# The last batch of a long-convolution kernel: its inverse transform cut by time instead of by channel

## The chip, the cores and the metric

The kernel runs on one core of a Trainium2 chip. The metric is the device time of one execution, in microseconds.

## The reference, cut to what matters

For each of 8 batches, linear attention without softmax on 8 heads of 64 channels over 576 positions, normalised by its root mean square, gives `x` (576 x 512). Then a gated long convolution:

```python
proj = x @ w_proj                                   # 512 -> 3 * 512
x1, x2, x3 = proj[..., :D], proj[..., D:2*D], proj[..., 2*D:]
X2 = np.fft.rfft(x2, n=S, axis=1)                   # S = 576
H = np.fft.rfft(filter_fft, n=S, axis=0)[None]
x2_conv = np.fft.irfft(X2 * H, n=S, axis=1)
out = (x1 * x2_conv * x3) @ w_out                   # float32, 8 x 576 x 512
```

## The kernel before

Matrices are bf16, sums and output float32. Both transforms are matrix multiplications with tables made on the chip. The spectrum of a batch is `Y`, six tiles of frequencies by 512 channels: three groups g (0, 1, 2), each with two parts h (0 even, 1 odd). `fft(b, g)` makes group g: TensorE transforms, VectorE (DVE) multiplies with the filter's spectrum (L423, L424), and an add joins the halves: on GpSimd (POOL) for g = 1 (L426), on DVE through the returned function for g = 0 of batches 1 to 7 (L427); group 2 is one multiply (L432). `proj13` makes the gate `g13` = x1 * x3, four channel groups of 128 (matmuls L443, DVE multiply L449).

The inverse, `inv(b, dcs)`, works on channel groups `dcs` with channels on partitions and time along the free axis, in a fixed order: position c of 576 stands for block c // 64, and a block's 64 positions are rows three apart in time. For a channel group TensorE makes an odd and an even half of 288 columns in PSUM (192 from groups 1 and 2, L469; 96 from group 0, L471). ScalarE (ACT) copies the odd half to SBUF (L473), DVE adds and subtracts the halves (L475, the second one reversed, L478) into `u`, three more DVE steps over thirds of 192 (L481, L483, L482) give the convolution `w`, and a multiply with `g13` (L487) gives `yg`.

The output projection needs all 512 channels (`yg` of all four groups) of a block: `outp` does 256 positions (blocks 0 to 3, 4 to 7) in one PSUM tile (matmuls L505, ACT copy L513) and issues transfers of 256 KB from SyncE's queue (SP, L516); block 8 of two batches shares a tile (L509).

Batches overlap: while b is projected and inverted, b + 1 runs its attention. The last batch has none, and `last(b)` ends the kernel by another scheme: the inverse runs one channel group at a time, the two output tiles of the batch before stand between the groups, and then `out1` makes five tiles of 128 positions: first the mixed tile (block 8 of batches 6 and 7, L530), then blocks 0 and 1, 2 and 3, 4 and 5, 6 and 7 (L527). Each is evicted by ACT or DVE (L533) and leaves in two transfers of 128 KB, one on SP and one on POOL, SP or ACT's queue (L536).

PSUM is four rotating tiles of two banks (`ps_tile`); SBUF work tiles rotate by tag. The framework derives waits from tiles and regions, and its scheduler orders each engine's instructions.

Of the kernel before, what the change touches and what calls it, by code (L numbers as in the profile page):

```python
# [9 lines left out]
FP32 = mybir.dt.float32  # L10
BF16 = mybir.dt.bfloat16
# [4 lines left out]
P = 128  # L16
# [4 lines left out]
def kernel(  # L21
# [16 lines left out]
    nc = tc.nc  # L38
    B, H, S, D = q.shape
    DM = H * D  # L40
    D3 = 3 * DM
    assert (B, H, S, D) == (8, 8, 576, 64)
    SB = S // 3
# [12 lines left out]
    def ps_tile(name):  # L56
        return psp.tile([P, 2, 512], FP32, name=name, tag="ps")
# [345 lines left out]
    def fft(b, g):  # L403
        x2 = st[b]['x2']
        if g == 1:
            st[b]['Y'] = work.tile([P, 6, DM], BF16, name="Y", tag="Y")
        Y = st[b]['Y']
        xp = ps_tile("ps_X")
        mm = nc.tensor.matmul
        lo, hi = slice(0, 64), slice(64, P)  # L410
        if g < 2:
            n = N1 if g == 0 else P
            if g == 0:
                mm(xp[:n, 0], FW[0:96, 0, 0, 0:n], x2[0:96, 0], start=True, stop=True)
                for c in range(2):
                    mm(xp[:n, 1], FX[:, c, 0:n], x2[:, c], start=(c == 0), stop=(c == 1))
            else:
                for ri in range(2):
                    mm(xp[:, ri], FW[:, 0, 2 + ri], x2[:, 2 + ri], start=True, stop=False)
                mm(xp[:, 0], FW[lo, 1, 2], x2[lo, 4], start=False, stop=True)  # L420
                mm(xp[:, 1], FX[hi, 2], x2[hi, 4], start=False, stop=True)  # L421
            t_ = work.tile([P, 2, 2, DM], FP32, name="tpw", tag="tpw", bufs=2)
            nc.vector.tensor_mul(out=t_[:n, 0], in0=xp[:n], in1=HH[:n, g, 1:3])  # L423
            nc.vector.tensor_mul(out=t_[:n, 1], in0=xp[:n], in1=HH[:n, g, 0:2])  # L424
            if g or not b:
                nc.gpsimd.tensor_add(out=Y[:n, 2 * g:2 * g + 2], in0=t_[:n, :, 0], in1=t_[:n, :, 1])  # L426
            return lambda: nc.vector.tensor_add(out=Y[:n, 2 * g:2 * g + 2], in0=t_[:n, :, 0], in1=t_[:n, :, 1])  # L427
        for i, r in enumerate((lo, hi)):
            mm(xp[r, 0], FW[:, 0, 4 + i, r], x2[:, 2 + i], start=True, stop=False)
        mm(xp[lo, 0], FW[lo, 1, 4, lo], x2[lo, 4], start=False, stop=True)  # L430
        mm(xp[hi, 0], FX[hi, 3, hi], x2[hi, 4], start=False, stop=True)
        nc.vector.tensor_mul(out=Y[:, 4:6], in0=xp[:, 0:1].to_broadcast([P, 2, DM]), in1=HM)  # L432
# [18 lines left out]
    def inv(b, dcs):  # L451

        Y, g13 = st[b]['Y'], st[b]['g13']
        if dcs[0] == 0:
            st[b]['yg'] = work.tile([P, NDC, S], BF16, name="yg", tag="yg", bufs=3)
        m = len(dcs)
        if m == 2:
            po, pe = ps_tile("ps_invo"), ps_tile("ps_inve")  # L460
            p_ = (pe[:, :, 0:TH], po[:, :, 0:TH])
        else:
            pp = ps_tile("ps_inv")
            p_ = (pp[:, 0:1, 0:TH], pp[:, 1:2, 0:TH])
        for h in (1, 0):
            for i, dc in enumerate(dcs):
                cs = slice(dc * P, (dc + 1) * P)
                for g in (1, 2):
                    nc.tensor.matmul(p_[h][:, i, 0:SB], Y[:, 2 * g + h, cs], IV[:, 2 * g + h, 0:SB],  # L469
                                     start=(g == 1), stop=(g == 2))  # L470
                nc.tensor.matmul(p_[h][:, i, SB:TH], Y[:N1, h, cs], IV[:N1, h, 0:SB // 2], start=True, stop=True)  # L471
        os_ = work.tile([P, 2, TH], FP32, name="os", tag="os")[:, 0:m]
        nc.scalar.copy(out=os_, in_=p_[1])  # L473
        u = work.tile([P, 2, S], BF16, name="u", tag="u", bufs=2)[:, 0:m]
        add = nc.vector.tensor_add(out=u[:, :, 0:TH], in0=p_[0], in1=os_)  # L475
        if b == 0:
            tc.keep_in_program_order(add)
        nc.vector.tensor_sub(out=u[:, :, TH:S], in0=p_[0][:, :, ::-1], in1=os_[:, :, ::-1])  # L478
        w = work.tile([P, 2, S], BF16, name="w", tag="w", bufs=2)[:, 0:m]
        u3, w3 = (t.rearrange("p j (m r) -> p j m r", m=3) for t in (u, w))  # L480
        nc.vector.tensor_add(out=w3[:, :, 1], in0=u3[:, :, 0], in1=u3[:, :, 2])  # L481
        nc.vector.tensor_sub(out=w3[:, :, 1], in0=u3[:, :, 1], in1=w3[:, :, 1])  # L482
        nc.vector.tensor_add(out=w3[:, :, 0:3:2], in0=u3[:, :, 0:3:2], in1=u3[:, :, 1:2].to_broadcast([P, m, 2, SB]))  # L483
        d2 = slice(dcs[0], dcs[0] + m)

        def fin():
            nc.vector.tensor_mul(out=st[b]['yg'][:, d2], in0=w, in1=g13[:, d2])  # L487
        return fin
# [3 lines left out]
    def o_rows(b, *blks):  # L492
        t0 = [SB * (x // 3) + x % 3 for x in blks]
        two = [[(t0[1] - t0[0]) * DM, 2]] if len(t0) == 2 else []
        return bass.AP(tensor=out.tensor, offset=out.offset + (b * S + t0[0]) * DM, ap=[[3 * DM, 64]] + two + [[1, DM]])
# [21 lines left out]
                else:  # L517
                    nc.sync.dma_start(out=o_rows(b - 1 + i, NR - 1), in_=ot[64 * i:64 * i + 64, 0])

    def out1(b, c, ev, q1):  # L520

        yg = st[b]['yg']
        pp = ps_tile("ps_out")
        for dc in range(NDC):
            kw = dict(start=(dc == 0), stop=(dc == NDC - 1))
            if c < 4:
                nc.tensor.matmul(pp[:, 0], yg[:, dc, c * P:(c + 1) * P], wo[:, dc], **kw)  # L527
            else:
                for i, y in enumerate((yt[0], yg)):
                    nc.tensor.matmul(pp[64 * i:64 * i + 64, 0], y[:, dc, 4 * P:S], wo[:, dc], **kw)  # L530
        ot = work.tile([P, 2, DM], FP32, name="ot", tag="ot", bufs=3) if c < 3 else \
            work.tile([P, 2, 2, DM], FP32, name="ot_", tag="tpw", bufs=2)[:, 0]
        ev(out=ot[:, 0], in_=pp[:, 0])  # L533
        for i in range(2):
            bb, blk = (b, 2 * c + i) if c < 4 else (b - 1 + i, NR - 1)
            (q1 if i else nc.sync).dma_start(out=o_rows(bb, blk), in_=ot[64 * i:64 * i + 64, 0])  # L536

    def last(b):
        for dc in range(NDC):
            inv(b, (dc,))()  # L540
            if dc < 2:
                outp(b - 1, 2 * dc)
        act, dve = nc.scalar.copy, nc.vector.tensor_copy
        for c, ev, q1 in ((4, act, nc.gpsimd), (0, dve, nc.gpsimd), (1, act, nc.sync), (2, act, nc.scalar), (3, dve, nc.scalar)):
            out1(b, c, ev, q1)


    def warm(n):
# [22 lines left out]
    for b in range(B):  # L571
        nxt = b + 1 < B
        proj2(b)
        if b == 1:
            fins.append(inv(0, (2, 3)))
            fins[0]()
        if b:
            fins[1]()
        if b == 0:
            fold_filter()  # L580
            proj13(0, 0)
            proj13(0, 1)
            gen_h(1)
            gen_h(0)
            fft(0, 1)
            gen_h(2)
            qtr(1, (0,))
            fft(0, 0)
            qtr(1, (1,))
            fft(0, 2)  # L590
            kv(1)
        elif nxt:
            kv(b + 1)
            qtr(b + 1)
        if b + 2 < B:
            load_kv(b + 2, (0, 8))
            load_q(b + 2)
        if b == 0:
            proj13(0, 2)
            att_o(1, 0)  # L600
            att_o(1, 1)
            att_r(1, 0)
            att_r(1, 1)
            att_o(1, 2)
            proj13(0, 3)
            att_x(1, 0)
            fold(1, 0)
            att_o(1, 3)
            att_r(1, 2)
            att_r(1, 3)  # L610
            att_x(1, 1)
            fold(1, 1)
            fins = [inv(0, (0, 1))]
        for dc in range(NDC) if b else ():
            if dc < 3:
                add = fft(b, (1, 0, 2)[dc]) or add
            if nxt:
                att_o(b + 1, dc)
            proj13(b, dc)
            if dc == 2:  # L620
                add()
            if nxt:
                att_r(b + 1, dc)
                if dc % 2:
                    att_x(b + 1, dc // 2)
                    fold(b + 1, dc // 2)
            if b and nxt and dc in (1,):
                outp(b - 1, 2 * (1,).index(dc))
        if not nxt:
            last(b)  # L630
            continue
        if b:
            for c0 in (2, 4):
                outp(b - 1, c0)
            del st[b - 1]
            fins = [inv(b, (dp, dp + 1)) for dp in (0, 2)]
            fins[0]()
# [30 lines left out]
```

## Time and profile before

| | us |
|---|---|
| median of 6 runs (234.9 to 235.37) | 234.94 |
| the profiled execution's own time | 234.93 |
| its span, first to last instruction | 232.8 |
| busy: TensorE | 211.1 (91%) |
| busy: DVE | 196.0 (84%) |
| busy: ACT | 156.7 (67%) |
| busy: POOL | 70.5 (30%) |
| projections of the last batch end on TensorE (L443) | 214.09 |
| last multiply with the gate (L487) ends | 223.64 |
| last TensorE result | 225.85 |

All times below count from the start of the span. TensorE's clock was granted at 0.99 of full speed over the span. The engine shares are means over the whole kernel; the change is in the last twenty microseconds, and what counts there is read from that stretch.

### The profile page before, as it was taken

Reading aid. Unit: us, or ns where it says so; the run is one execution under the profiler, and the core shown is the slowest. Engines: PE = TensorE matmul, PEld = TensorE weight load, DVE = VectorE, ACT = ScalarE, POOL = GpSimd, SP = SyncE. Lnnn points to the kernel's source line nnn. Section 1 sums busy time; section 2 is a strip of 40 time slices with the busy share of each in tenths; the row PEclk is TensorE's granted clock in tenths of the full one; section 3 lists DMA queues with packets and bytes.
Section 4 is the critical chain, followed back from the end, with each engine's and each line's share of the span. In section 5 each row is a group of like instructions: output and inputs, shape, how many; then the busy total and the mean of one; then the engine's idle time right before and its main releaser. Section 6 shows DMA issues by size and latency. Waiting matters only on the chain.

```text
span 232.8 us, 4866 instructions
## 1 busy us (share of the span) xinstructions
PE 211.1 (91%) x1951; PEld 127.8 (55%) x1951; DVE 196.0 (84%) x380; ACT 156.7 (67%) x232; POOL 70.5 (30%) x86
## 2 busy tenths in 40 slices
PE   4967789879998999999999999999999999999960
PEld 1433355645565575756675666656675666567420
DVE  6978687898996989798989899788979897999860
ACT  2748927866876696868785987679676977532520
POOL 7984454951630074005600470004000300030010
PEclk9999999999999999999999999999999999999995
DMA  5999999999993369743992299230113002500446
GB/s 62 152 187 233 236 193 198 189 193 176 140 174 93 90 75 184 140 120 45 170 198 53 51 171 207 43 106 1 36 57 90 3 17 76 135 0 3 103 120 183
DMA packets 45544, 27.38 MB, mean 118 GB/s; under 512 B 22242, under 2 KB 40674, under 8 KB 45522
## 3 DMA queue, kind: packets, MB, share of 16 engines
q0 software_dynamic: 40240, 17.90, 60.3%
q1 hardware_dynamic: 5122, 8.92, 14.8%
q8 instruction: 15, 0.25, 0.4%
q10 hardware_dynamic: 160, 0.26, 0.4%
q14 instruction: 7, 0.06, 0.1%
HBM read 33.88 MB, written 9.44 MB: 186 GB/s over the span
## 4 chain that ended last, share of the span: by engine, by line
PE 65%; ACT 14%; POOL 6%; DMA 6%; DVE 4%; issue 2%; POOLq 0%; DVEq 0%
PE ps_x L443 21%; PE ps_out L505 10%; DMA fc<-in_moe_filter_fft_dram,fidx 6%; PE ps_x L393 5%; ACT qT L288 5%; PE ps_o L297 3%; PE ps_x L384 3%; PE ps_r L312 2%; PE ps_x L399 2%; ACT sq L298 2%; PE ps_invo L469 2%; ACT kvblk L266 2%; PE ps_kv L255 2%; PE ps_inve L469 2%; PE ps_x L387 2%
## 5 line engine op out<-in xcount | busy, mean ns | idle before, releaser
L443 PE MATMUL ps_x<-x,wp 128*128 128x288 bf16 x512 | 67.8, 286 | 0.6 <-ACT rstd L313 0.6
L443 PEld LDWEIGHTS <-wp 128*128 128x128 bf16 x512 | 49.7, 98 | 14.5 <-issue 1.8
L426 POOL TENSOR_TENSOR Y<-tpw 128x1024 bf16<-128x1024 f32 (+1 forms) x9 | 21.2, 2356 | 70.2 <-PE ps_x L443 43.2
L449 DVE TENSOR_TENSOR g<-ps_x,x 128x576 bf16<-128x576 f32 x32 | 24.0, 753 | 10.5 <-ACT x L447 8.2
L313 ACT ACTIVATE rstd<-ps_r,bias_eps 128x576 bf16<-128x576 f32 x32 | 23.2, 739 | 5.4 <-PE ps_r L312 5.3
L505 PE MATMUL ps_out<-wo,yg 128*128 128x512 bf16 x112 | 26.6, 379 | 0.0
L447 ACT CAST x<-ps_x 128x576 bf16<-128x576 f32 x32 | 20.7, 646 | 8.8 <-PE ps_x L443 8.8
L70 POOL DMA_DIRECT2D km<-in_k_dram x9 | 8.0, 884 | 61.5 <-PE ps_kv L255 58.3
L298 ACT ACTIVATE sq<-ps_o 128x576 bf16<-128x576 f32 x32 | 20.5, 652 | 7.2 <-PE ps_o L297 7.0
L513 ACT COPY ot<-ps_out 128x1024 f32<-128x1024 f32 (+1 forms) x17 | 15.9, 937 | 13.8 <-PE ps_out L505 13.8
L423 DVE TENSOR_TENSOR tpw<-ps_X,HH 128x1024 f32<-128x1024 f32 (+1 forms) x16 | 19.6, 1222 | 5.1 <-PE ps_X L421 4.6
L424 DVE TENSOR_TENSOR tpw<-ps_X,HH 128x1024 f32<-128x1024 f32 (+1 forms) x16 | 19.4, 1213 | 0.0
L303 ACT ACTIVATE osb<-ps_o,g_col 128x576 bf16<-128x576 f32 x25 | 18.5, 742 | 0.0
L393 PE MATMUL ps_x<-wp,ab 128*128 128x512 bf16 x64 | 15.9, 381 | 2.2 <-DVE ab L339 2.2
L505 PEld LDWEIGHTS <-yg 128*128 128x128 bf16 x112 | 10.8, 98 | 10.4
L473 ACT COPY os<-ps_invo 128x576 f32<-128x576 f32 x14 | 9.0, 643 | 9.8 <-PE ps_x L387 5.1
L297 PE MATMUL ps_o<-qT,kvblk 128*128 128x288 bf16 x64 | 12.6, 286 | 3.2 <-DVE kvblk L264 1.2
L288 ACT COPY qT<-ps_qT 128x1152 bf16<-128x1152 bf16 x14 | 15.0, 1122 | 0.1
L312 PE MATMUL ps_r<-sq,ind 128*128 128x288 bf16 x64 | 13.0, 285 | 1.5 <-ACT sq L298 1.0
L79 POOL DMA_DIRECT2D qb<-in_q_dram x16 | 12.6, 795 | 1.5 <-POOLq L652 0.8
L321 DVE TENSOR_TENSOR x<-osb,rstd 128x1152 bf16<-128x1152 bf16 x16 | 12.1, 754 | 0.9 <-ACT rstd L313 0.8
L552 PE MATMUL ps_w<-kvblk,ind 128*128 128x512 bf16 x33 | 9.5, 429 | 3.7 <-DVE ind L103 3.4
(192 smaller groups left out, 408.8 us busy)
## 6 DMA issues: line engine op xcount, KB each, us to landing
out_dram<-ot SPq DMA_DIRECT2D x28, 256.0 KB, 3.3
qb<-in_q_dram POOLq DMA_DIRECT2D x16, 288.0 KB, 8.4
km<-in_k_dram POOLq DMA_DIRECT2D x7, 512.0 KB, 7.0
vm<-in_v_dram POOLq DMA_DIRECT2D x7, 512.0 KB, 8.1
wp<-in_moe_w_proj_dram POOLq DMA_DIRECT2D x3, 512.0 KB, 12.3
out_dram<-ot SPq DMA_DIRECT2D x10, 128.0 KB, 3.3
fa<-in_moe_filter_fft_dram POOLq DMA_DIRECT2D x1, 672.0 KB, 14.8
km<-in_k_dram POOLq DMA_DIRECT2D x2, 256.0 KB, 5.3
```

The lines of the kernel that those rows point to most:

```text
L288: nc.scalar.copy(out=o_, in_=i_)
L297: nc.tensor.matmul(op[:, h, 0:TH], kvblk[b % 2][:, j], s['qT'][:, 2 * (j % 2) + j // 2, h * TH:(h + 1) * TH], start=True, stop=True)
L298: nc.scalar.activation(out=s['sq'][:, j].rearrange("p (a b) -> p a b", a=2), in_=op[:, :, 0:TH], func=AF.Square)
L313: nc.scalar.activation(out=s['rstd'][:, j].rearrange("p (a b) -> p a b", a=2), in_=r2[:, :, 0:TH], func=AF.Abs_reciprocal_sqrt, scale=1.0 ...
L393: nc.tensor.matmul(pp[:, h], ab[:, j, h * SB:h * SB + P], wp[:, j, DM:2 * DM], start=(j == 0), stop=(j == NDC - 1))
L423: nc.vector.tensor_mul(out=t_[:n, 0], in0=xp[:n], in1=HH[:n, g, 1:3])
L424: nc.vector.tensor_mul(out=t_[:n, 1], in0=xp[:n], in1=HH[:n, g, 0:2])
L426: nc.gpsimd.tensor_add(out=Y[:n, 2 * g:2 * g + 2], in0=t_[:n, :, 0], in1=t_[:n, :, 1])
L443: nc.tensor.matmul(pp[:, h, 0:TH], w_, x[:, j, h * TH:(h + 1) * TH], start=(j == 0), stop=(j == NDC - 1))
L447: nc.scalar.copy(out=x1, in_=pp[:, :, 0:TH])
L449: nc.vector.tensor_mul(out=st[b]['g13'][:, dc].rearrange("p (a b) -> p a b", a=2), in0=pp[:, :, 0:TH], in1=x1)
L505: nc.tensor.matmul(pp[:, cc], yg[:, dc, c * P:(c + 1) * P], wo[:, dc], start=(dc == 0), stop=(dc == NDC - 1))
```

## The change

`last(b)` no longer walks over the channel groups. For all four groups at once it makes the first 128 of the 192 columns and the 96 (224 columns, odd then even, L551 and L553, in two PSUM tiles), and then the remaining 64 of the 192 (L557, a third PSUM tile). Blocks 0, 1, 7 and 8 depend on the 224 columns alone: their sums and their multiplies with the gate (L574, L575) are written first; the middle blocks 2 to 6 follow (L577 to L586) with one multiply over 320 positions (L588). The batch before's two output tiles stand behind the inverse. The tiles of `out1` are now blocks 0 and 1, blocks 7 and 8, block 6 with block 8 of the batch before, blocks 2 and 3, blocks 4 and 5; the engines and queues that evict and send them are reassigned. In `fft`, the add of group 0 of the last batch is on POOL too. Lines L551 to L588 are numbered as in the changed kernel, all others as before.

```diff
@@ -422,8 +422,9 @@
             t_ = work.tile([P, 2, 2, DM], FP32, name="tpw", tag="tpw", bufs=2)
             nc.vector.tensor_mul(out=t_[:n, 0], in0=xp[:n], in1=HH[:n, g, 1:3])
             nc.vector.tensor_mul(out=t_[:n, 1], in0=xp[:n], in1=HH[:n, g, 0:2])
-            if g or not b:
+            if g or b in (0, B - 1):
                 nc.gpsimd.tensor_add(out=Y[:n, 2 * g:2 * g + 2], in0=t_[:n, :, 0], in1=t_[:n, :, 1])
+                return
             return lambda: nc.vector.tensor_add(out=Y[:n, 2 * g:2 * g + 2], in0=t_[:n, :, 0], in1=t_[:n, :, 1])
         for i, r in enumerate((lo, hi)):
             mm(xp[r, 0], FW[:, 0, 4 + i, r], x2[:, 2 + i], start=True, stop=False)
@@ -517,32 +518,84 @@
                 else:
                     nc.sync.dma_start(out=o_rows(b - 1 + i, NR - 1), in_=ot[64 * i:64 * i + 64, 0])
 
-    def out1(b, c, ev, q1):
-
-        yg = st[b]['yg']
+    def out1(b, c0, ev, ot, qs):
+
+        yg, blk = st[b]['yg'], c0 // 64
         pp = ps_tile("ps_out")
         for dc in range(NDC):
             kw = dict(start=(dc == 0), stop=(dc == NDC - 1))
-            if c < 4:
-                nc.tensor.matmul(pp[:, 0], yg[:, dc, c * P:(c + 1) * P], wo[:, dc], **kw)
+            if blk != 6:
+                nc.tensor.matmul(pp[:, 0], yg[:, dc, c0:c0 + P], wo[:, dc], **kw)
             else:
-                for i, y in enumerate((yt[0], yg)):
-                    nc.tensor.matmul(pp[64 * i:64 * i + 64, 0], y[:, dc, 4 * P:S], wo[:, dc], **kw)
-        ot = work.tile([P, 2, DM], FP32, name="ot", tag="ot", bufs=3) if c < 3 else \
-            work.tile([P, 2, 2, DM], FP32, name="ot_", tag="tpw", bufs=2)[:, 0]
-        ev(out=ot[:, 0], in_=pp[:, 0])
+                for i, y in enumerate((yg[:, dc, c0:c0 + 64], yt[0][:, dc, 4 * P:S])):
+                    nc.tensor.matmul(pp[64 * i:64 * i + 64, 0], y, wo[:, dc], **kw)
+        ev(out=ot, in_=pp[:, 0])
         for i in range(2):
-            bb, blk = (b, 2 * c + i) if c < 4 else (b - 1 + i, NR - 1)
-            (q1 if i else nc.sync).dma_start(out=o_rows(bb, blk), in_=ot[64 * i:64 * i + 64, 0])
+            qs[i].dma_start(out=o_rows(b, blk + i) if blk != 6 or i == 0 else o_rows(b - 1, NR - 1),
+                            in_=ot[64 * i:64 * i + 64])
 
     def last(b):
-        for dc in range(NDC):
-            inv(b, (dc,))()
-            if dc < 2:
-                outp(b - 1, 2 * dc)
+
+
+        Y, g13 = st[b]['Y'], st[b]['g13']
+        yg = st[b]['yg'] = work.tile([P, NDC, S], BF16, name="yg", tag="yg", bufs=3)
+        dv, HB = nc.vector, SB // 2
+        M = P + HB
+        tiles = {1: ps_tile("ps_invo"), 0: ps_tile("ps_inve")}
+        pb = ps_tile("ps_invb")
+        for h in (1, 0):
+            for dc in range(NDC):
+                cs, c0 = slice(dc * P, (dc + 1) * P), dc % 2 * M
+                pp = tiles[h][:, dc // 2]
+                for g in (1, 2):
+                    nc.tensor.matmul(pp[:, c0:c0 + P], Y[:, 2 * g + h, cs], IV[:, 2 * g + h, 0:P],
+                                     start=(g == 1), stop=(g == 2))
+                nc.tensor.matmul(pp[:, c0 + P:c0 + M], Y[:N1, h, cs], IV[:N1, h, 0:HB], start=True, stop=True)
+        for h in (1, 0):
+            for dc in range(NDC):
+                for g in (1, 2):
+                    nc.tensor.matmul(pb[:, h, dc * 64:(dc + 1) * 64], Y[:, 2 * g + h, dc * P:(dc + 1) * P],
+                                     IV[:, 2 * g + h, P:SB], start=(g == 1), stop=(g == 2))
+        osa = work.tile([P, 2, 2 * M], FP32, name="osa", tag="tpw", bufs=2)
+        osb_ = work.tile([P, NDC * 64], FP32, name="osb_", tag="os")
+        nc.scalar.copy(out=osa, in_=tiles[1][:, :, 0:2 * M])
+        nc.scalar.copy(out=osb_, in_=pb[:, 1, 0:NDC * 64])
+
+        ua = work.tile([P, NDC, 2 * M], BF16, name="ua", tag="sq")
+        ub = work.tile([P, NDC, 2, 64], BF16, name="ub", tag="u", bufs=2)
+        w = work.tile([P, NDC, S], BF16, name="wl", tag="osb")
+        e4, o4 = (t[:, :, 0:2 * M].rearrange("p k (i c) -> p k i c", i=2) for t in (tiles[0], osa))
+        u4 = ua.rearrange("p (k i) c -> p k i c", i=2)
+        dv.tensor_add(out=u4[:, :, :, 0:M], in0=e4, in1=o4)
+        dv.tensor_sub(out=u4[:, :, :, M:2 * M], in0=e4[:, :, :, ::-1], in1=o4[:, :, :, ::-1])
+        r = lambda a, z: ua[:, :, P + a:P + z]
+        s2 = lambda a, z: ua[:, :, P + a + SB - 64:P + z + SB - 64]
+        for c, x, y in ((0, ua[:, :, 0:P], r(0, P)), (SB * 2 + 64, s2(64, SB), r(64, SB))):
+            dv.tensor_add(out=w[:, :, c:c + P], in0=x, in1=y)
+            dv.tensor_mul(out=yg[:, :, c:c + P], in0=w[:, :, c:c + P], in1=g13[:, :, c:c + P])
+        wm = w[:, :, SB:2 * SB]
+        dv.tensor_sub(out=wm[:, :, 64:SB], in0=r(64, SB), in1=s2(64, SB))
+        dv.tensor_sub(out=wm[:, :, 64:P], in0=wm[:, :, 64:P], in1=ua[:, :, 64:P])
+        dv.tensor_sub(out=wm[:, :, 0:64], in0=r(0, 64), in1=ua[:, :, 0:64])
+        e3, o3 = pb[:, 0, 0:NDC * 64].rearrange("p (j c) -> p j c", c=64), osb_.rearrange("p (j c) -> p j c", c=64)
+        dv.tensor_add(out=ub[:, :, 0], in0=e3, in1=o3)
+        dv.tensor_sub(out=ub[:, :, 1], in0=e3[:, :, ::-1], in1=o3[:, :, ::-1])
+        ends = w[:, :, SB:SB + 2 * P].rearrange("p j (x c) -> p j x c", c=P)[:, :, :, 0:64]
+        dv.tensor_sub(out=ends, in0=ends, in1=ub[:, :, ::-1])
+        rr_ = ua[:, :, P:3 * P].rearrange("p j (x c) -> p j x c", c=P)[:, :, ::-1, 0:64]
+        dv.tensor_add(out=w[:, :, 64:S].rearrange("p j (x c) -> p j x c", c=2 * P)[:, :, :, 64:P], in0=ub, in1=rr_)
+        mid = slice(P, 7 * 64)
+        dv.tensor_mul(out=yg[:, :, mid], in0=w[:, :, mid], in1=g13[:, :, mid])
+        for c in (0, 2):
+            outp(b - 1, c)
         act, dve = nc.scalar.copy, nc.vector.tensor_copy
-        for c, ev, q1 in ((4, act, nc.gpsimd), (0, dve, nc.gpsimd), (1, act, nc.sync), (2, act, nc.scalar), (3, dve, nc.scalar)):
-            out1(b, c, ev, q1)
+        q0, q1, q2 = nc.sync, nc.scalar, nc.gpsimd
+        ot = lambda tag, bufs: work.tile([P, 4, DM] if tag == "tpw" else [P, 2, DM] if tag == "ot" else [P, 3, DM],
+                                         FP32, name="ot_", tag=tag, bufs=bufs)[:, 0]
+        for c0, ev, tag, bufs, qs in ((0, act, "ot", 3, (q0, q2)), (7 * 64, act, "tpw", 2, (q0, q2)),
+                                      (6 * 64, dve, "ff", 1, (q0, q1)), (2 * 64, act, "ot", 3, (q0, q1)),
+                                      (4 * 64, dve, "tpw", 2, (q0, q1))):
+            out1(b, c0, ev, ot(tag, bufs), qs)
 
 
     def warm(n):
@@ -613,11 +666,11 @@
             fins = [inv(0, (0, 1))]
         for dc in range(NDC) if b else ():
             if dc < 3:
-                add = fft(b, (1, 0, 2)[dc]) or add
+                add = fft(b, (1, 0, 2)[dc]) or (dc and add)
             if nxt:
                 att_o(b + 1, dc)
             proj13(b, dc)
-            if dc == 2:
+            if dc == 2 and add:
                 add()
             if nxt:
                 att_r(b + 1, dc)
```

## The prediction

> **What bounds the kernel now.** The change touches only the last batch (b = 7), so the views are read from the back: first the chain of waits over the last stretch, then the timeline of the output queues there, then the busy table by microsecond, then the groups by shape for prices.
>
> ```profile
> 223.70 0.40 PE ps_out L530
> 224.10 1.75 PE ps_out L527 x7
> 225.85 0.02 issue
> 225.88 0.69 DVE ot__3319 L533
> ```
>
> The chain ends with the output projection of batch 7, which could start in earnest only when the last channel group's multiply (L487, 223.18 to 223.64) had made the last quarter of `yg`. All five output tiles were released together by it. The queues show what follows:
>
> ```profile
> 225.38 3.61 SPq L536 DMA_DIRECT2D out_dram<-ot  x4
> 225.62 0.56 POOL L536 DMA_DIRECT2D out_dram<-ot  x1
> 225.78 0.55 ACTq L536 DMA_DIRECT2D out_dram<-ot  x1
> 226.60 0.51 ACTq L536 DMA_DIRECT2D out_dram<-ot__3319  x1
> 229.08 0.55 SPq L536 DMA_DIRECT2D out_dram<-ot__3319  x1
> ```
>
> The last eviction ends at 226.57, but SP is still issuing (one of its issues took 1.49 us where others take 0.54) and gets to the last transfer at 229.08.
>
> ```profile
> 218.00:219.00 1.00, 1.00 (x13) 0.87 (x12) 0.97 (x5) 0.58 (x1) 0.00 (x0) 1.00 0.42 90
> ...
> 222.00:223.00 1.00, 0.89 (x5) 0.42 (x6) 0.97 (x5) 0.00 (x0) 0.00 (x0) 1.00 0.72 240
> 223.00:224.00 1.00, 1.00 (x5) 0.20 (x2) 0.60 (x2) 0.00 (x0) 0.00 (x0) 1.00 0.01 4
> 224.00:225.00 1.00, 1.00 (x5) 0.41 (x5) 0.54 (x1) 0.82 (x2) 0.00 (x0) 1.00 0.02 8
> 225.00:226.00 1.00, 0.84 (x4) 0.19 (x2) 0.27 (x2) 0.75 (x2) 0.94 (x2) 1.00 0.07 16
> 226.00:227.00 1.00, 0.00 (x0) 0.00 (x0) 0.57 (x1) 0.00 (x0) 0.17 (x1) 1.00 0.97 229
> ...
> 230.00:231.00 1.00, 0.00 (x0) 0.00 (x0) 0.00 (x0) 0.00 (x0) 0.00 (x0) 0.50 0.78 250
> ```
>
> The last two columns (DMA share, GB/s) tell why: the DMA engines idle from 223 to 226 and are then full to 231. So the end is a drain: ten transfers of 131 KB, 1.31 MB, at 257 GB/s (mean of the five windows 226 to 231). The span ends 1.65 us after the drain (231.15 to 232.8), and the execution's 234.93 us is 2.13 more than its span; that is the median of the runs (234.94) within 0.01.
>
> **The change part by part.** Work before 210.4 us stands in the same order on every engine, so I carry the clock from there.
>
> *The add of group 0.* It leaves DVE (L427, 1.22 us at 212.91) for POOL. POOL's row for it is 2.36 us; its input (L424) ends at 210.42, so Y is complete at 212.8. TensorE reaches the inverse at 214.09, behind its projections: 1.3 us of cover, cost 0; without it TensorE would wait one for one. POOL has nothing else queued before the output transfers. DVE gains nothing either: the next thing it does is the L449 at 214.19, which waits for TensorE.
>
> *The inverse on TensorE.* 8 groups of 128 + 128 + 96 columns and 16 matmuls of 64: 3840 columns, as before, but 40 matmuls for 24. Three matmuls of 480 columns take 0.21 us now, 0.44 ns a column, so the 24 large ones take 1.23. For 64 columns no row has this weight shape; bounds are 27 ns (columns alone) and 98 ns (a whole weight load record). I take 45: in the chain the L469 after a 96-column L471 starts 45 ns after it, so a 128x128 weight load fits in that. 16 x 45 = 0.72. End: 214.09 + 1.95 = 216.04. Range 215.75 to 218.0 (all 40 at 98 ns).
>
> The Trainium skill ("TensorE: Matmul & The Clock Gate", Back-to-back issue gap) speaks against cutting matmuls small: it gives some 81 ns a matmul at 128 columns in a stream of load and multiply. By that the inverse would take 40 x 81 ns = 3.24 us, 1.3 more, with everything behind it later by as much; the 45 ns spacing in this trace is well under it.
>
> *The eviction and the DVE chain.* The odd half (1408 columns, 0.62) is there at 214.71. ACT copies 896 elements: 0.402 for 288 and 1.012 for 1024 give 0.91, to 215.65. DVE's two f32 steps of 896: 0.455 for 288 and 0.752 for 576 give 1.08 each; a following independent instruction starts 0.08 before the end of the last, a dependent one 0.03 after it. They end at 217.75. The bf16 steps (0.258 for 192, 0.350 for 384, 0.752 for 1152) cost 0.29 for 256 elements, 0.42 for 512, 0.82 for 1280. In the built order: L579 217.78; the two adds 217.99 and 218.33; the two multiplies 218.67 and 219.01. So `yg` of blocks 0, 1 is ready at 219.09, of 7, 8 at 219.43. Then L577 219.35, L581 219.69, L578 220.03, L582 220.24 to 220.66, L584 220.69, L586 221.03 to 221.45, and the 1280-wide multiply (L588) 221.48 to 222.30. Before, the last multiply ended at 223.64. The bound from below is the same chain without start overheads, some 0.5 less; from above, bf16 at the f32 price (5376 elements x 0.52 ns), 2.8 more.
>
> *TensorE behind it.* The previous batch's two output tiles (L505, 1.74 each) now stand behind the whole inverse: 216.04 to 219.52; before, the first ended at 216.24. They hide DVE's chain: blocks 0, 1 start at 219.52, 0.43 after their data, and end at 220.39. Blocks 7, 8 need the PSUM slot that L582 frees: 220.71 to 221.58. The mixed tile of block 6 and the previous batch's block 8 is next and waits for L588, its batch-6 half queued behind that wait too: 222.35, a stall of 0.77, and 0.98 for its eight matmuls (as L509), to 223.33. Two more tiles at 0.87, with 0.17 for the last result: 225.24. DVE evicts (0.69) to 225.96. So the last transfers can be issued at 226.0, by SP and ACT at once, instead of 226.60 and 229.08.
>
> *The transfers.* Now SP has five of the last ten, ACT three, POOL two. ACT's first issue stands between its evictions (0.55, waiting for DVE's copy at 224.1): the tile of blocks 2, 3 is evicted 0.3 late, off the chain, because blocks 4, 5 are later. But the previous batch's tiles leave later: first eviction 217.81 to 218.82, issue 218.86 instead of 217.31, first bytes 1.2 later as before, 220.05. From there the queues always hold something: by 225.4, 1.57 MB have been offered and 1.37 drained. So the whole 2.36 MB (four of 262 KB, ten of 131 KB) drains in one stretch: 2.36 / 0.257 = 9.18 us, to 229.23. At 277 GB/s (best window) 228.6; at 239 (mean of 219 to 223, SP's queue alone) 229.9. If draining did not bind, the last issue would: 226.0 + 1.2 + 0.26 MB / 0.257 = 228.2.
>
> The Trainium skill ("DMA: Bandwidth & Descriptors", Anatomy of one DMA) puts the moving part of a transfer at bytes / 436 GB/s. By that the stretch would take 5.4 us, draining would not bind, and the last issue would set the end; no window here passes 290 GB/s, so the measured rate stands in the sum.
>
> *Sum.* 229.23 + 1.65 = 230.9 span, + 2.13 = 233.0 us. Between the drain rates it runs from 232.35 to 233.7, and the last issue gives 232.0; the later half of the drain uses three queues, for which the windows 227 to 230 show 252 to 277, so I take 232.8: the drain ends 2.1 us earlier than 231.15.
>
> **The rivals.**
>
> *The last issue sets the end, not the drain (231.7 to 232.2).* It needs over 290 GB/s over nine microseconds, or an earlier start. For it: single quarter-microsecond slices at 350. Against: no whole window over 287.
>
> *Small matmuls space out (234.1 to 234.8).* At 81 to 98 ns each, the previous batch's first tile leaves 1.3 to 2 us later and the drain with it: 234.1 to 234.8. For it: average spacing of weight loads in the inverse now is 70 ns, and nothing proves 27 to 45 in a row. Against: the 45 ns step above. The result is a small gain or none that shows. DVE at the f32 price in all bf16 steps ends alike: last issue 228.8, end 231.05, 234.8.
>
> *Slower: DVE pays for each short run.* The new steps walk 64 pieces in all, many of 64 elements, between L569 and L588, and that chain now gates five of nine blocks at once. Each piece's price lands on the last issue. To be slower than before by what a measurement can tell (0.2%, 0.47 us) the last issue must slip by 3.4 us, L588 ending at 225.7: 53 ns a piece. At 80 ns: 5.1 us, 237. For it: no row has runs of 64. Against: L338 (two runs of 96, one reversed) takes 0.248, L482 (one of 192) 0.250: nothing a piece.
>
> *The change doesn't do what it says.* The built order shows that it does: the outputs of blocks 0, 1, 7, 8 stand on TensorE ahead of the mixed tile. What could fail is timing: if blocks 0, 1 start after 222, nothing leaves early; that is the case of slow DVE above.
>
> **How the numbers follow.** The drain case 0.62, the last issue 0.13, spaced matmuls or unpacked bf16 0.15 (two thirds of it still faster by over 0.2%, one third within), DVE by piece or another stall of that size 0.10 (0.08 slower). Faster 0.85, same 0.06, slower 0.09 (same is within 0.2% of 234.94: 234.47 to 235.41). Range 231.8 to 234.6: it takes in the drain, the issue bound and most of the spaced case; above it lie some 0.13, below some 0.05.
>
> **What would show it.** Right: POOL's second add ends near 212.8 and TensorE doesn't wait for it; the inverse ends near 216.0; L588 ends near 222.3; a TensorE stall of about 0.8 before the mixed tile; last eviction near 226.0; DMA share 0.9 or more from 220 to 229 without a hole; span 230.7. Wrong: L557 spaced by more than 50 ns, L574 to L588 steps over their prices, or a hole in the DMA share between 222 and 226, which would say that issue and not draining binds.

## The result and the profile after

The changed kernel takes 233.69 us (median of 21 runs) against 235.05 (47 runs): a ratio of 0.9929, 95% interval 0.9911 to 0.9947, some 1.7 us faster (1.4 by the medians). The ratio goes by the fast runs of both kernels alone, so it isn't the quotient of the two medians (0.9942). A second set of runs gave 0.9915 (0.9887 to 0.9943). The profiled execution took 233.59 us with a span of 231.5.

The first 210 us differ by up to 3.5 us from one profiled execution to the next, with the same instructions. So single profiles are compared by their *tail*: from the start of the last batch's first POOL add (L426), before which nothing is changed, to the end of the span. It is 232.8 - 207.66 = 25.14 before and 231.5 - 207.92 = 23.58 after (23.44 in the second profile), 1.6 less, which agrees with the runs. Times of the profile after stand 0.26 later than those of before at equal progress. Line numbers in a view are those of the kernel that it shows.

The chain of waits of the changed kernel, two cuts of its end:

```profile
214.34 0.11 PE ps_invo L551 x2
...
215.05 0.91 ACT osa L561
...
221.65 0.83 DVE yg L588
222.48 0.04 issue
222.53 1.05 PE ps_out L531 x8
223.58 1.85 PE ps_out L528 x8
...
225.52 0.69 DVE ot__3310 L532
```

Three tiles and not five stand behind the last multiply (L588); between ACT's copy and it the chain runs over DVE alone. TensorE in the timeline (in brackets: how long the engine was idle before, and what ended it):

```profile
215.44 0.63 PE L557 MATMUL ps_invb<-IV,Y 128*128 128x64 bf16 x16
215.91 3.62 PE L506 MATMUL ps_out<-wo,yg 128*128 128x512 bf16 x16
219.37 1.89 PE L528 MATMUL ps_out<-wo,yg 128*128 128x512 bf16 x8
222.53 1.05 PE L531 MATMUL ps_out<-wo,yg 128*64 128x512 bf16 x8 [1.27 <-DVE yg L588]
```

The two early tiles (219.37) follow the previous batch's without a gap; then there is a stall of 1.27 us. The output queues in the timeline, which answer to the SP and ACT lines shown of before:

```profile
...
223.10 1.15 SPq L534 DMA_DIRECT2D out_dram<-ot__3279  x1
224.35 1.74 SPq L534 DMA_DIRECT2D out_dram<-ot__3288  x1
...
226.18 0.68 SPq L534 DMA_DIRECT2D out_dram<-ot__3301  x1
226.24 0.77 ACTq L534 DMA_DIRECT2D out_dram<-ot__3310  x1
227.21 0.47 SPq L534 DMA_DIRECT2D out_dram<-ot__3310  x1
```

The last eviction ends at 226.21, and ACT issues at once; SP, held in 1.15 and 1.74 us issues, a microsecond later. The busy table by microsecond (its last columns: granted clock, DMA share, GB/s):

```profile
219.00:220.00 1.00, 1.00 (x6) 0.36 (x5) 1.00 (x4) 0.43 (x1) 0.00 (x0) 1.00 0.00 0
220.00:221.00 1.00, 1.00 (x6) 0.39 (x4) 0.96 (x4) 1.00 (x2) 0.00 (x0) 1.00 0.85 174
...
222.00:223.00 1.00, 0.47 (x6) 0.27 (x8) 0.47 (x1) 0.00 (x0) 0.53 (x1) 1.00 0.73 203
223.00:224.00 1.00, 1.00 (x9) 0.35 (x6) 0.38 (x1) 0.00 (x0) 0.00 (x0) 1.00 0.68 195
224.00:225.00 1.00, 1.00 (x6) 0.45 (x5) 0.31 (x1) 0.00 (x0) 0.00 (x0) 1.00 1.04 309
...
229.00:230.00 1.00, 0.00 (x0) 0.00 (x0) 0.00 (x0) 0.00 (x0) 0.00 (x0) 0.50 0.53 184
```

The idle microseconds 223 to 226 of before are gone: the DMA engines work from 220.1 to 229.7 in one stretch, 2.36 MB in 9.6 us (246 GB/s), with a dip of the share to 0.73 and 0.68 from 222 to 224. The dip is not for want of issued transfers: 1.31 MB had been issued by 222.7 (SP's four large ones and POOL's two), and 0.80 MB had left by 224 (sum of the windows from 220).

### The profile page after: what moved, and what is told of

Its sections match the earlier page's. It is cut to its first block, busy times and chain, and to the rows that moved or that the text cites. A ratio compares the mean times of both kernels' runs of the same rounds, so it can differ in the third digit from the quotient of the medians.

```text
span 231.5 us, 4883 instructions
## 1 busy us (share of the span) xinstructions
PE 211.2 (91%) x1967; PEld 128.2 (55%) x1967; DVE 193.9 (84%) x369; ACT 156.7 (68%) x230; POOL 73.0 (32%) x87
## 4 chain that ended last, share of the span: by engine, by line
PE 63%; ACT 14%; DVE 7%; POOL 6%; DMA 6%; issue 2%; POOLq 0%; DVEq 0%; ACTq 0%
PE ps_x L444 21%; PE ps_out L506 9%; DMA fc<-in_moe_filter_fft_dram,fidx 6%; PE ps_x L393 5%; ACT qT L288 5%; PE ps_x L384 3%; PE ps_o L297 3%; PE ps_x L399 2%; PE ps_r L312 2%; ACT sq L298 2%; PE ps_invo L470 2%; PE ps_kv L255 2%; PE ps_inve L470 2%; PE ps_x L387 2%; ACT kvblk L266 2%
## 5 line engine op out<-in xcount | busy, mean ns | idle before, releaser
L426 POOL TENSOR_TENSOR Y<-tpw 128x1024 bf16<-128x1024 f32 (+1 forms) x10 | 23.6, 2356 | 70.7 <-PE ps_x L444 43.2
L424 DVE TENSOR_TENSOR tpw<-ps_X,HH 128x1024 f32<-128x1024 f32 (+1 forms) x16 | 19.4, 1213 | 0.0
L605 PE MATMUL ps_w<-kvblk,ind 128*128 128x512 bf16 x33 | 10.9, 480 | 3.7 <-DVE ind L103 3.4
```

## The experiments

Three theories on what sets the end now: the *drain* (all bytes from the first transfer on, at some 250 GB/s), the *last issue* (the last eviction and its transfers, the rest hidden), and *SP's queue* (its slow issues). All kernels below are edits of the changed one; tails are to be set against the changed kernel's two, 23.58 and 23.44. Each tail is that of one profile.

**The changed kernel again.** 

> The changed kernel as it is, as the mark for the others. All theories: about 0.993 of the kernel before, 233.5 us; last multiply with the gate ends near 222.5, last landing near 230.3, span 231.5.

233.45 us, ratio 0.9915; tail 23.44; time, span (231.5) and last multiply (ends at 222.6) as expected. SP's last issue comes at 227.48.

**Without the previous batch's output transfers.**

```diff
+                if n == 2 and ...:        # the two calls in last() alone
+                    continue
                 if n == 2:
                     nc.sync.dma_start(...)
```

> The four 256 KB transfers of the previous batch's output (blocks 0 to 7 of batch 6) are left out, everything else stays. Drain theory (the end is 2.36 MB drained at about 250 GB/s from the first of these transfers on): only 1.31 MB is left, never more than a tile or two waiting, so the last issue sets the end: span some 1.2 to 1.6 shorter, 232.2 us. Last-issue theory (evictions set the end, the bytes are hidden): no change, 233.5. SP-queue theory (SP's issues of 1.0, 1.15 and 1.74 us hold back the last transfer to 227.2): these issues fall back to 0.55 and the last transfer is issued at 226.2, 1.0 earlier: 232.5. So this run tells the last-issue theory from the other two.

Measured: 232.48 us, ratio 0.9897 (0.985 to 0.9943); tail 22.40, 1.1 less. The last eviction stands where it stood (18.3 us after the POOL add in both), so the last-issue theory falls: bytes that leave earlier do set the end. SP's issues fall to 0.47 us, and its last comes at once:

```profile
226.12 0.47 SPq L536 DMA_DIRECT2D out_dram<-ot__3306  x1
226.13 0.74 ACTq L536 DMA_DIRECT2D out_dram<-ot__3306  x1
```

**The last two tiles' SP halves on POOL's queue.**

```diff
-  (2 * 64, act, "ot", 3, (q0, q1)), (4 * 64, dve, "tpw", 2, (q0, q1))
+  (2 * 64, act, "ot", 3, (q2, q1)), (4 * 64, dve, "tpw", 2, (q2, q1))
```

> The SP halves of the last two tiles (blocks 2, 3 and 4, 5) go out on POOL's queue, which is idle then, instead of SP's. SP-queue theory: the last transfer is issued at 226.2 and not 227.2, so 0.7 to 1.0 faster. Drain theory: the bytes are the same, 0 to 0.2 faster. Last-issue theory: the last eviction is the same, 0 to 0.3 slower through POOL's longer way (3.0 to 3.3 to landing for its transfers before against 2.5).

Measured: 233.52 us, ratio 0.9922 (0.9895 to 0.9948): no change; tail 23.92. The last transfer is issued 0.7 to 0.8 earlier (18.6 instead of 19.3 to 19.4 after the POOL add), and nothing comes of it: the tail is 0.3 to 0.5 above the changed kernel's, where the drain theory had 0 to 0.2 less. The timeline and the busy table of this kernel:

```profile
227.16 0.53 POOL L534 DMA_DIRECT2D out_dram<-ot__3310  x1
```

```profile
229.00:230.00 1.00, 0.00 (x0) 0.00 (x0) 0.00 (x0) 0.00 (x0) 0.00 (x0) 1.00 0.86 252
230.00:231.00 1.00, 0.00 (x0) 0.00 (x0) 0.00 (x0) 0.00 (x0) 0.00 (x0) 1.00 0.24 84
```

The engines still work 3.5 us after that issue (2.5 in the kernel without the previous batch's transfers): the drain lasts from 220.8 to 230.7, 9.9 us. SP's slow issues are a sign of the backlog: without those transfers they took 0.47. This run alone doesn't rule out that they also set the end, for POOL's way is longer (there 2.7 and 3.0 us from issue to landing against SP's 2.3), which takes back most of what the earlier issue gains. The last pair of kernels below decides it.

**The last multiply twice.**

```diff
         dv.tensor_mul(out=yg[:, :, mid], in0=w[:, :, mid], in1=g13[:, :, mid])
+        dv.tensor_mul(out=yg[:, :, mid], in0=w[:, :, mid], in1=g13[:, :, mid])
```

> The last multiply with the gate (five middle blocks, 0.82 us) is done twice, so TensorE, the evictions and the issues of the last three tiles come 0.83 later. Last-issue theory: 0.8 slower. Drain theory: the transfers already waiting cover it, up to some 0.3 slower. SP-queue theory: SP is late anyway, its last issue moves by less than half: 0 to 0.4 slower.

Measured: 233.83 us, ratio 0.9949 (0.9922 to 0.9976), tail 24.76: over the drain's bound, and its last eviction came 2.4 later for a multiply of 0.83. The chain and the busy table show why:

```profile
223.51 1.05 PE ps_out L531 x8
224.57 3.43 PE ps_out L528 x8
```

```profile
224.00:225.00 1.00, 1.00 (x8) 0.34 (x5) 0.39 (x1) 0.00 (x0) 0.00 (x0) 0.82 0.92 274
225.00:226.00 1.00, 1.00 (x3) 0.29 (x2) 0.30 (x1) 0.00 (x0) 0.00 (x0) 0.50 1.01 254
```

TensorE waited 2.13 us, and its granted clock fell to half just when the last two tiles ran: 3.43 us instead of 1.85. Seven of the twelve runs lie between 233.2 and 233.9, near the changed kernel, and five from 234.6 up, so by the times it doesn't seem to happen in every run. So this run could not tell the theories apart, and was repeated with the clock kept up.

**The same, with TensorE kept busy in the wait.**

```diff
+            if c0 == 6 * 64:
+                warm(9)
             out1(b, c0, ev, ot(tag, bufs), qs)
```

> The last multiply done twice as before, and nine matmuls without use (1.9 us) stand on TensorE in the wait that this makes, so that it is never idle for 2 us there. If the half clock seen after that wait is caused by the idle time: clock 1.00 up to the last matmul, 1.85 and not 3.43 us for the last eight matmuls, last eviction near 227.0, and what remains above the changed kernel is the uncovered part of the 0.83: 0.1 to 0.4. If the clock has another cause: the half clock stays in some of the runs.

Measured: 233.85 us, ratio 0.9926 (0.9893 to 0.996). Its profiled execution was 2.8 us late at the POOL add already, so only its tail is used: 23.51, nothing above the changed kernel, though the last eviction ends 0.86 later. The timeline:

```profile
226.16 1.05 PE L531 MATMUL ps_out<-wo,yg 128*64 128x512 bf16 x8 [0.19 <-DVE yg L589]
227.15 1.90 PE L528 MATMUL ps_out<-wo,yg 128*128 128x512 bf16 x8
```

1.90 us for the last eight matmuls, and beside the profiled run only one of the other twelve is above 234.5 (five of twelve were, without the added matmuls): so the lost clock was the idle time's doing. And 0.83 us more on the chain cost nothing: the drain covers it.

**The last multiply in three parts, block 6 first.**

```diff
-        (ends -= ub; blocks 2, 6 = ub + rr_; one multiply over 320)
+        (blocks 2, 6 = ub + rr_; ends -= ub; multiplies of block 6, blocks 2-3, blocks 4-5)
```

> The last multiply over 320 positions is cut in three, block 6 first, so that the mixed tile can start about 0.5 us earlier and the last eviction ends 0.4 to 0.5 earlier. Last-issue theory: 0.4 faster than the changed kernel. Drain theory: the bytes and their start are the same, 0 to 0.15 faster.

Measured: 233.76 us, ratio 0.9938 (0.9906 to 0.997), tail 23.66. The last eviction ends 0.65 earlier, and SP's last issue 0.8 to 0.9 *later*:

```profile
225.69 0.69 DVE L532 COPY ot__3312<-ps_out 128x512 f32<-128x512 f32 x1 [1.21 <-PE ps_out L528]
...
228.93 0.47 SPq L534 DMA_DIRECT2D out_dram<-ot__3312  x1
```

No gain (the tail is 0.1 to 0.2 above the changed kernel's), as the drain theory says: what is made sooner waits longer.

**The early blocks last, without and with TensorE kept busy.**

```diff
-  0, 7 * 64, 6 * 64, 2 * 64, 4 * 64      # places, engines and queues stay in order
+  6 * 64, 2 * 64, 4 * 64, 0, 7 * 64
```

> The five last tiles in another order: the mixed tile, blocks 2 and 3, 4 and 5, and only then 0 and 1, 7 and 8, which are ready early; engines and queues stay with their place in the order. TensorE then waits about 3 us for the last multiply (219.6 to 222.5) and has all five tiles behind it (4.5 us), last eviction near 228. If the early departure is what the change brings: the queues run empty near 224.5, 1.31 MB are still to come, time 2.0 or more above the changed kernel, level with before or slower; if TensorE's clock falls in the wait, as it did where the last multiply was done twice, up to 4 more. If the gain lies in the shorter DVE chain instead: at most 1 above the changed kernel.

> The early blocks last, with twelve matmuls without use (2.6 us) in TensorE's wait of 3.0 us before the mixed tile, so that the clock stays full. If early departure is worth something by itself: five tiles behind the last multiply, last eviction near 227.6, the queues empty for a microsecond or more around 225, 1.0 to 1.5 us above the changed kernel. If the whole loss of that order was the clock: level with the changed kernel.

Measured: 235.88 us, ratio 1.0012 (0.9972 to 1.0051), tail 26.10 without; 234.86 us, ratio 0.9999 (0.9974 to 1.0023), tail 24.46 with the added matmuls. The first lost the clock after a wait of 3.00 us (1.92 us for the mixed tile's matmuls instead of 1.05):

```profile
222.31 1.92 PE L531 MATMUL ps_out<-wo,yg 128*64 128x512 bf16 x8 [3.00 <-DVE yg L588]
```

```profile
222.00:223.00 1.00, 0.69 (x4) 0.36 (x6) 0.25 (x1) 0.00 (x0) 0.00 (x0) 0.64 0.60 182
```

The second shows the order alone: 0.9 to 1.0 over the changed kernel in the tail, with the hole that was expected:

```profile
224.00:225.00 1.00, 1.00 (x6) 0.47 (x5) 0.00 (x0) 0.58 (x2) 0.47 (x1) 1.00 0.37 137
225.00:226.00 1.00, 1.00 (x7) 0.47 (x5) 0.52 (x1) 0.24 (x1) 0.56 (x2) 1.00 0.62 121
```

So by the tails about 1.0 of the 1.6 us is the early departure of four blocks, and some 0.7 would be there with all five tiles behind the last multiply (25.14 to 24.46). By whole times nothing is left of the gain in this order (0.9999), and 0.6 us (0.9974) is the most that the interval allows. So the early departure is worth from 1.0 us up to the whole gain; what the rest is worth isn't settled.

**The add of group 0 back on DVE.**

```diff
-            if g or b in (0, B - 1):
+            if g or not b:
-                add = fft(b, (1, 0, 2)[dc]) or (dc and add)
+                add = fft(b, (1, 0, 2)[dc]) or add
```

> The add of group 0 of the last batch goes back to DVE (1.2 us), the rest of the change stays. All theories that see it as covered: same as the changed kernel, 0.991 to 0.993 of before; the inverse's first group-0 matmul may wait some 0.05 for it, since DVE's add ends near 214.4. Rival, that POOL's add disturbs DVE or TensorE: 0.2 or more faster than the changed kernel.

Measured: 233.85 us, ratio 0.9942 (0.9904 to 0.9979), tail 23.41: the move to POOL is worth nothing and costs nothing that shows.

**The previous batch's tiles earlier.** First one ahead of the whole inverse and one inside it, with the multiply in three parts; then only the first tile, inside the inverse; then that, with no transfer on POOL.

```diff
+        outp(b - 1, 0)                     # ahead of the inverse's first matmul
...
+        outp(b - 1, 2)                     # ahead of the 64-column matmuls
```

> As the one before, and the previous batch's two output tiles leave earlier: the first stands ahead of the inverse on TensorE (eviction from 216.0 instead of 217.8), the second between the inverse's large matmuls and the 64-column ones. All of the inverse and the DVE chain come 1.74 later, so the last eviction ends about 1.2 later than in the changed kernel, near 227.4. Drain theory: with 0.52 MB gone early, the last issue and the drain end about together, 0.4 to 0.8 faster than the changed kernel. Last-issue theory: 1.2 slower.

Measured: 234.0 us, ratio 0.9934 (0.9899 to 0.997), tail 23.98: no gain, where 0.4 to 0.8 was expected. ACT's copy of the first tile (217.71 to 218.72) stood before its copy of the odd half (218.61), the inverse came 1.7 later, and the last eviction 1.3; the DMA share fell to 0.23 from 222 to 223 and 0.44 from 225 to 226. So the drain no longer bound; the last issue did, by the figures: from the last issue to the end this kernel takes 4.3 us, as do the kernel without the previous batch's transfers (4.1) and the one with the early blocks last (4.3), more than the 3.9 of the prediction (2.2 to the end of the transfers, 1.65 to that of the span).

```diff
+        outp(b - 1, 0)                     # ahead of the 64-column matmuls
         for h in (1, 0):
...
-        for c in (0, 2):
-            outp(b - 1, c)
+        outp(b - 1, 2)
```

> The previous batch's first output tile stands between the large matmuls of the inverse and the 64-column ones (0.47 us), so the first transfer is issued 0.45 earlier; the DVE chain, the last multiply and the last eviction stay where they are. Drain theory: 0.3 to 0.45 faster than the changed kernel. Last-issue theory: no change.

Measured: 233.02 us, ratio 0.9888 (0.9833 to 0.9943), tail 23.11. First issue 0.47 earlier, last eviction unmoved (18.29 after the POOL add in both), end 0.3 to 0.5 earlier: the drain's start carries over to the end. SP's last issue also came 0.4 to 0.5 earlier, and the changed kernel, too, ends 4.0 to 4.3 us after it; so this run alone doesn't tell the drain from SP's queue.

```diff
-  (0, ..., (q0, q2)), (7 * 64, ..., (q0, q2))
+  (0, ..., (q0, q1)), (7 * 64, ..., (q0, q1))
```

> As the one before, with the two transfers of the early tiles that went out on POOL's queue on ACT's queue instead. In the changed kernel the DMA share falls to 0.7 from 222 to 224, just when POOL's transfers run. If they cause that hole: the drain is 0.3 to 0.5 shorter, 0.6 to 0.9 faster than the changed kernel. If not: as the one before, or slower by up to 0.5, since ACT's issues stand between its evictions and can be held back as SP's are.

Measured: 232.75 us, ratio 0.9879 (0.9824 to 0.9933), tail 22.34, the best of all: 1.1 to 1.2 less than the changed kernel. (By whole times its interval overlaps the changed kernel's, and it is only 0.3 below the step before, which these few runs can't tell apart.) SP's last issue stands 18.91 after the POOL add in this kernel and in the one before:

```profile
226.10 0.47 SPq L534 DMA_DIRECT2D out_dram<-ot__3310  x1
```

```profile
227.37 0.56 SPq L534 DMA_DIRECT2D out_dram<-ot__3310  x1
```

The last eviction, too, ends 18.29 after it in both, and still the tail is 0.77 shorter: the last SP transfer took 2.3 us from issue to landing, for 2.9. So neither the last eviction nor SP's queue set the end of the kernel before; the drain did. In this kernel the dip is gone:

```profile
222.00:223.00 1.00, 0.00 (x0) 0.00 (x0) 0.97 (x2) 0.59 (x1) 0.00 (x0) 1.00 0.89 268
223.00:224.00 1.00, 0.94 (x8) 0.37 (x8) 0.01 (x1) 0.00 (x0) 0.00 (x0) 1.00 0.98 246
```

2.36 MB drain in 9.1 us (220.2 to 229.3, 259 GB/s), and the end follows 1.5 us later instead of 1.8. That POOL's transfers make the dip is not shown cleanly: the step before had them, and a share of 0.86 to 0.88 there.

## Why the prediction was right, point by point

*The add on POOL, cost 0.* Right. It ended at 213.10, TensorE's L553 came at 214.29; the run with the add back on DVE agrees.

*The inverse, 1.95 us.* It took 1.73 (214.18 to 215.91). The 24 large matmuls took 1.26 (1.23 predicted); the 16 of 64 columns start 29 ns apart (0.47 in all), the lower bound and not the 45 taken. So the rival of spaced matmuls fell. The Trainium skill's 81 ns ("TensorE: Matmul & The Clock Gate", Back-to-back issue gap) is not seen here: two matmuls of 128 columns take 0.11 us in the chain, and the measurement decides.

*The DVE chain, 6.63 us from L569 to the end of L588.* 6.49 (215.99 to 222.48); runs of 64 elements cost nothing a piece, so the slower rival fell.

*The PSUM wait of blocks 7 and 8 on L582.* This step failed: the eight matmuls of the early tiles run through in 1.89 us from 219.37, so the second tile starts before L582 (220.41 to 220.82) has ended; it doesn't wait for that slot. The 0.3 saved here and the 0.2 at the inverse only made the stall longer (1.27 for 0.77), so the miss had no effect.

*The last eviction at 225.96.* 226.21, which is 225.95 with the 0.26 of the start taken off.

*The last transfers by SP and ACT at once at 226.0.* Wrong for SP, which came 0.97 after ACT; the profile of before had shown the same 1.49 us issue under load, and I left it out. In the last pair of kernels, one step away from this one, it didn't set the end.

*The drain.* The mechanism was right: 0.83 us more on the chain is free, an earlier chain is worth nothing, a start 0.47 earlier is worth 0.3 to 0.5, fewer bytes are worth 1.1. The other bound, the last issue, lies 1.1 us lower (tail 22.40 without those bytes); a last eviction 1.3 us later (the first kernel with earlier tiles) or 1.7 us later (the early blocks last, TensorE kept busy) is no longer covered.

The size was off. The drain took 9.6 us at 246 GB/s where 9.18 at 257 stood in the sum (0.42 more), and the span ended 1.8 us after it for 1.65 (0.15 more). The first byte, at 220.1, only looks on time: with the 0.26 of the start taken off it came 0.2 early, mostly by the shorter inverse. Together with the 0.26 that makes a span of 231.5 for 230.9. The last choice, taking 232.8 instead of the sum's 233.0 because of the faster windows, went the wrong way. So 1.7 us were gained, by the ratio, where 2.1 were forecast.

*The sign "a DMA share of 0.9 or more from 220 to 229 without a hole".* It failed: the share was 0.73 and 0.68 from 222 to 224 and 0.74 from 228 to 229. The prediction would have read a hole there as issue and not draining being the limit. That reading was wrong: transfers were waiting during the dip, and the last pair of kernels shows the drain setting the end. But a rate taken from another stretch knows nothing of such dips; here it was 4% too high.

The 436 GB/s of the Trainium skill ("DMA: Bandwidth & Descriptors", Anatomy of one DMA), which the page fits to single transfers issued from POOL's queue, are far from what any of these drains showed (238 to 259 GB/s).

## What to carry to other kernels

When the end of a kernel is a burst of stores, add up the bytes still to leave, divide by the rate that the profile shows under load, and count from the first store, not from the last eviction: while the engines are full, shortening the chain that makes the last tile brings nothing, and starting the first store earlier brings about what it is earlier. Work out the other bound as well, the last issue and what follows it (4.1 to 4.3 us here): it takes over as soon as the drain is shortened or the chain gets later. Spread the last stage by the axis along which results become complete, so that stores can leave before the rest is computed. When such a reordering makes TensorE wait (here 2.13 and 3.00 us cost clock, 1.77 and less did not), look at the granted clock after the wait before blaming the order.

## What the runs showed of the hardware that was not expected

What a wait costs TensorE's clock can come after the wait. After 2.13 us of idle time (221.4 to 223.5) the clock was still 1.00 for a microsecond of work and fell to 0.50 about 3.2 us after the idle time began; after 3.00 us (219.3 to 222.3) it fell right at the end of the wait (0.64 over the window 222 to 223). In both kernels it stayed low for some 3.4 us (224.6 to 228.1, 222.3 to 225.7, worked out from the shares of the windows). The delay is not fixed: at the ends of the kernels, where TensorE simply stops, the clock falls between 2.1 us after its last result (the changed kernel, 225.4 and 227.5) and 5.0 us after it (the kernel with the last transfers on POOL's queue, 226.1 and 231.1). That fits a wait of 2.13 us that costs something in only some of the runs. Waits of 1.27 to 1.29 us left the clock at 1.00 in all seven profiles that have one, and so did 1.77 us in the one profile with it. So the price of a wait can fall on matmuls that run well behind it, here 1.6 us for 0.83 us of delay.

SP's issue of one transfer takes 0.47 us with an empty queue and up to 1.75 with several transfers before it, and a transfer's time from issue to landing rose from 2.3 us (without the previous batch's transfers) to 5.5 in the backlog. Where the drain set the end, the slow issues cost nothing.
